# Sliding-window attention with a gated feed-forward block: the first two pairs of query tiles worked by halves of their heads, and the written order planned again

## The chip, the cores and the metric

The kernel runs on one NeuronCore of a Trainium2 chip. The core has five engines that each follow their own list of instructions: TensorE (PE in the profile; PEld is its weight load), VectorE (DVE), ScalarE (ACT), GpSimd (POOL) and SyncE (SP), which here only issues transfers. The metric is the device time of one execution in microseconds. Eleven executions of the kernel before have a median of 258.07 us, from 257.2 to 260.35.

## The reference

The reference is causal attention over q, k, v of shape (4 batches, 8 heads, 768 positions, 64), followed by a gated feed-forward block. Heads 0, 2 and 6 see every earlier position. The other five see the first 4 positions (the sinks) and a window of 64.

```python
scores = scale * np.matmul(q, k.transpose(0, 1, 3, 2))
# mask: causal for heads 0, 2, 6; causal and (sink or window) for the others
a = np.exp(scores - np.max(scores, axis=-1, keepdims=True))
a = a / (np.sum(a, axis=-1, keepdims=True) + 1e-09)
x = np.matmul(a, v)                     # (4, 8, 768, 64) -> (3072 tokens, 512)
g = x @ w_gate                          # 512 -> 1536
out = (g / (1 + np.exp(-g)) * (x @ w_val)) @ w_out
```

## The kernel before

**Tiles and pairs.** A query tile is 128 positions of one batch with all 8 heads; there are 24. Tiles come in 12 pairs, because one load brings 256 positions: load q*n*, k*n*, x*n* (x is v) are 512 KB each. A pair goes through a cast to 16 bits (`cast`, tasks cq, ck), transposes on TensorE (`transposes`, tasks tr*n*.0 for q and tr*n*.1 for k) and evacuations from PSUM (`evacq` and `evack`, tasks evq and evk) into `qT` and `kT`. From pair 5 on, transfers that transpose (dq, dk) take the place of TensorE's transposes.

**A tile.** Each tile has units of scores (sc*t*.*u* on TensorE), an exponential on ScalarE (ex), for tiles from 4 on a multiplication with a mask (mask, VectorE or GpSimd), matmuls with the values for the odd heads and then for the even ones (val*t*.1, val*t*.0), a division by the row sum (rc and nm, VectorE), and a transposition into `xt` (xtr and xe, or from tile 8 on a transfer, xdma).

**Feed-forward.** Four tiles make a group of 512 tokens, six groups in all. For each of 12 blocks j of 128 hidden units there are four matmuls with the gate weights (`gate`, L778, task gate*g*.*j*), a tanh on ScalarE, one VectorE instruction that makes silu's first part (`stt1`, L788), four matmuls with the value weights (L778, task vals*g*.*j*), and one VectorE instruction that multiplies both (`stt2`, L795). Group 0 does its blocks 0 to 3 in two halves of 256 tokens. The output product (L813) follows. Weights are loaded by pieces of 512 KB (g, v and o, 0 to 5), and cast (tasks wc); piece v1 holds the value weights of blocks 2 and 3.

**PSUM.** The ring `gv` has three buffers. Both kinds of feed-forward matmul write there: a gate block gives its buffer back when `stt1` has read it, a value block when `stt2` has. So VectorE's pace sets when TensorE may start the next block. In the first two pairs k's transposes and some scores and value products use `gv` too. The rings `tr`, `sc` and `av` have one buffer each, and `raw`, where loads land, has 14.

**The order.** Nothing is scheduled when the kernel is built. Tasks are declared with what they need; `ORDER`, a string of two-digit numbers, gives the one sequence in which all are issued, and `WAYS` the engine of each task that has a choice. Both were written by a planner that isn't in the file. Each engine takes its tasks strictly in that sequence, SyncE its transfers too. Numbers from 3700 up are spare matmuls (`warm`) that compute nothing.

**Places.** `load` L311, `cast` L377, `transposes` L428, `evacq` L443, `evack` L448, `tasks_of_pair` L624, `tasks_of_tile` L687. The helpers `copy` (L175 on ScalarE, L177 on the others) and `recast` (L181, VectorE's cast, written as a reduction over one element) record most moves, so their lines gather several tiles.

Of the kernel before, what the change touches and what calls it, by code (L numbers as in the profile page):

```python
# [16 lines left out]
    "000802041L1M1T091O1V1Nxl1Y1W1U1Z1X1a0A01xj1b1c0B1p1t1q0C1Q0E1R1P1r031f0D1d2527262D280i1u1s1S1y2G"  # L17
    "0j2j1g2E1exi1i1h1n2H1o212I2F1j2A1k1l1v221z2J2K1w1x201mxh2L2M23290F24xh2p2N2O2P2q2V2W2r2Q2R102B9F"
    "2C2S9G159j2X2Z9Z2a112k0p2s169k2b9H0H2t2Y2c2d9a9b9P2x9l2e2T2y3Q9m9c2U2h9n0o2u2i9Q2v369R0I0k9o9d9p"
    "05063W3Y0G133A129q9I9J9S9T3B0q9r9s3D073X3E9K9L9M3R3Z3a9N30319e3C0K189O9t3M3b9f9y0n2w2m2l9u9g9v3c"  # L20
    "329h3e33192z9zA0A10L499i3F349U2o354F0t3f2n3G0l0JA29w1H2fAN3d9V3p0m9W4A4G4H9x3H1I0s3h37AO3IAS3J3i"
    "383KAT3t3u9XAP394I3L9YAQ4J3j3k1B3SA83N3V4K0r0M3O3g3TAR3lAV1E3m4L0NAUA9AA3zAW3n3oAI403wAJAD3xA30O"
    "3P41421F3q3U3v43AK443r3sALAEAFAM0v4NA41C3y45461K4WA54p4O4qAG4oAHA60PA747480yAB4Z4yBk4a2gACBlBmBn"
    "4PBVBoBWBG4c4wAwBXBHBI4d0xAzAx4Q4RAyB00u4BBfBgBhBiBjBJBK4M4C4S4TBQBR4xB6B7BS4v0w4f4gAu4E0zB8BTAr"
    "0R4l4DAs4z5014BUAtB1B24U4V0S17AX4YAv52Ba53Bb4uB31D1ABYAY0Y4b4e4X5D1G4r4h5758B90QBZ4i5G1JAZ5W5X5Z"
    "4jAaBABLB45e515H5JBM5V5K544kBc0TAc4mB5BB555IAdAe5f4s59BN5LBC56BO5M5N5cAf5d0U5A5BAhAi5O5P5C5E4t5Y"
    "5Q5RBEBPAg5g635F5S5h5iAjAk5r4nBDBd0X5T5U62615a5s5tAmAnAoBFCd5b6iAbCeAp6ABeCgCfCh69CYCZCOBpCPCQ5o"
    "5y6B68Aq0WBqBrCa5jBsCRCS5p6F6GC9CbCcCA5k5qBuCB0V0a6C6DCs6O6HBvCt6X6Y5uCu6h6l6gAl6m5vCvCw6UCiBt66"
    "6V6o6p5l6n5m64CjCkCl6q6E6RCJ6SCK6d5w5xCLCECm6I6J6TBw655n5zD26K0h8d600ZCT7PBx7XByBzCF6WD30b6u6v67"
    "6LC07W6MD46P6NCMCUCNCV6Q6r6sC16Z6aC2C3D5CHD66x6y6bCG6eCW757TCICx6cCX7879Cn7OCC6j6k7BC46t71Cy0gC5"  # L30
    "C6C7CzCDD0Co726fEA0d7C7N7V7UEBD7Cp0cCqCr6z70D1C8D86w737AEF747v8283EC7REGEH7g7hE0E57jE6E17tE27u7k"
    "D9DAEIEJE77D767I7J0f7SEDEEE8E97Q7EDgDR7FDhDSDT7GDCDD7H7YE37K7L0e7Z8a8h7lDEDiDbDeE481DcDU807i7q87"
    "7mDdDFDG88EKDH7nDV8YDy77DI7a7bDfDJDvDK7cELEMDLDw847o7pDMDxDq858A8B7rDW8G7z8c8MDNDO8Z8NDz7s7MDrDs"
    "DPDtDu868P8i7dDjDk7eDX8fDZ8QDYDa7w8JENEODl7x8gDm8CEPDnDo7fFSDpFTDB8D8KFU8V89FIFJ8EF3FL8pFKEyFMEz"
    "F0EQERES8H8F8eF1F88qF28OF9FA8mFDFEF4EU8L7y8R8S8nEVETF5DQFVFW8j8xF6F78kEW8lEX8r8s8T8U8WFGFFFH8oFc"
    "FdFNFOFP93948IEZEaFf8b8tEY8u90FeFg8X91EtEuEbEcEvFQ8vFB8w8z8y92EwFC989A99FXExFY969BEeFZ97Eo95Ep9C"
    "Fa9D9EFbEfEqEgEhFRErEsEjEkEmElEnGuGvGwGBGxGyFhGGGHGIEiGCGDGkGlGmFiGnGoFjGEGFGQFkGRGsFmFnGpGSEdGq"
    "GrGtFoFpFqG1G2GVGWG4G3G5G6GXFrFsGYGZGaGbGcFtFuGJGKG7GLGMFwFlG8FvG9GdGAFxGTGNGeGUGOGPGfFyGgFzGhGi"
    "GzH0GjH1G0H4H5H6H9HAHBHEHFHGH7H2H3H8HCHDHJHHHIHKHL"
)  # L40
WAYS = (
    "000000000000000000000000000000000000000000000000000000000000002022222222222222222210201212101000"
    "011000000100000000000000010001100202212210110100100001000000000000000200022220001101000000000000"
    "020000000000000010012220220000000100000000000100000000100000000012210220110000100000000011000100"
    "000000021010210210000000000000000002000010000000000002200120000000100000000001000010001210200000"
    "001001000000200001000000000000222020100000010010000000021000000100000000020122000000001000000000"
    "010000210020002200000000010000000200010000000000101222022000000100000000000000001000000000000000"
    "000000000000000000000000000000000000000000000000000000000000000000000000000000000000010000000000"
    "000000000000000000000000000000000000000000000000000000000000000010000000001000000000000000000000"
    "000000000000000000000000000000000000000000000000000000000000000000000000000000000000000000000000"  # L50
    "000000000000000000000000000000001000000000100000000000000000000000000000000000000000000000000000"
    "000000000000000010000000000000000000000000000000000000000000000000000000000000000000000000000000"
    "10000000000000000010"
# [52 lines left out]
def kernel(  # L106
# [204 lines left out]
    def load(kind, n):  # L311
        r = buf("raw", [128, 1024], FP, "raw")
        landed[kind, n] = r
        if kind in "qkx":
            b, pi = QP[n]
            sl = slice(pi * 256, (pi + 1) * 256)
            nc.sync.dma_start(  # L317
                out=r.rearrange("p (h x) -> p h x", h=H),
                in_={"q": q, "k": k, "x": v}[kind][b, :, sl, :].rearrange(
                    "h (p j) d -> p h (j d)", j=2))  # L320
        elif kind == "o":
            nc.sync.dma_start(
                out=r.rearrange("p (a n) -> p a n", a=2), in_=wod[:, 2 * n:2 * n + 2, :])
        else:
            nc.sync.dma_start(  # L325
                out=r.rearrange("p (a n) -> p a n", a=4),
                in_=(wgd if kind == "g" else wvd)[:, :, n * 256:(n + 1) * 256])

    T_load, T_iss = {}, {}
    for kd, n in ([(kd, n) for n in range(NP) for kd in "qkx"]  # L330
                  + [(kd, n) for kd in "gvo" for n in range(6)]):
        T_iss[kd, n] = P.add(f"load {kd}{n}", ["SP"], (lambda kd=kd, n=n: load(kd, n)),
                             takes=["raw"])
        T_load[kd, n] = P.lands(T_iss[kd, n])
# [42 lines left out]
    def cast(n, kd, x):  # L377
# [8 lines left out]
        if n not in hqs:  # L386
            h = buf("hq", [128, 2, 1024], FH, "hq")
            hqs[n] = [h[:, 0].rearrange("p (j r x) -> p j r x", j=2, r=2),
                      h[:, 1].rearrange("p (k a x) -> p k a x", k=2, a=4)]
        if kd == "k":  # L390
            ks = slice(0, 2) if x is None else slice(x, x + 1)
            recast(T_c[n, kd, x],
                 hqs[n][1][:, ks].rearrange("p k a (s d) -> p k s a d", s=2),
                 r.rearrange("p (k s r) j d -> p k s (r j) d", r=2, s=2)[:, ks])
            return
        js = slice(0, 2) if x is None else slice(x, x + 1)
        recast(T_c[n, kd, x],
             hqs[n][0].rearrange("p j r (k d) -> p k r j d", d=64)[:, :, :, js],
             r[:, :, js].rearrange("p (k r) j d -> p k r j d", r=2))
# [28 lines left out]
    def transposes(n, w):  # L428

        ring = "gv" if w and n < 2 else "tr"  # L430
        tr = buf(ring, [128, 4, 2, 2, 64] if w else [128, 2, 4, 128], FH, "tr")
        for j in range(2):
            for p in range(4):
                if w:
                    nc.tensor.transpose(tr[:, p, :, j, :], hqs[n][1][:, p // 2, p % 2 * 2 + j],
                                        ident)
# [4 lines left out]
        trs[n, w] = tr  # L441

    def evacq(n, s, x, ps):  # L443
        c = slice(s * 64, s * 64 + 64)
        copy(T_ev[n, s][x], qT[n % 2][c, s, ps].rearrange("c p j n -> c j p n"),
             trs[n, 0][c, :, ps])

    def evack(n, x, ps):  # L448
# [3 lines left out]
        copy(T_ev[n, 2][x],  # L452
             kT[b % 2][:, 2 * pi:2 * pi + 2].rearrange("c m k r x -> c (k r) m x")[:, ps],
             trs[n, 1][:, ps].rearrange("c p m j n -> c p m (j n)"))
# [169 lines left out]
    def tasks_of_pair(n):  # L624
# [5 lines left out]
        for kd in "qk":  # L630
            free = xqk and kd == "q"
            cs[kd] = []
            for x in range(2) if n < 2 or free else [None]:
# [3 lines left out]
                    deps=[T_load[kd, n]] + ([T_fill3] + T_dq.get(n - 1, []) if free else []),  # L637
# [24 lines left out]
        for w in range(xqk, 2 - xk):  # L662
            ring = "gv" if w and n < 2 else "tr"
            tr = P.add(f"tr{n}.{w}", ["PE"], (lambda n=n, w=w: transposes(n, w)),
                       deps=cs["qk"[w]], takes=[ring], after=[T_warm])
            cut = [slice(2, 4), slice(0, 2)] if n < 2 else [slice(0, 4)]
            evs = []
            if w:
                for x, ps in enumerate([slice(1, 4, 2), slice(0, 4, 2)] if n < 2 else cut):
                    evs.append(P.add(f"evk{n}.{x}", ["ACT", "DVE"],  # L670
                                     (lambda n=n, x=x, ps=ps: evack(n, x, ps)),
                                     deps=[tr] + older))
                T_ev[n, 2] = evs
            else:
                oldq = [x for t in (2 * n - 4, 2 * n - 3) if n > 1 for x in T_sc_of[TILES[t]]]
                T_ev[n, 0], T_ev[n, 1] = [], []
                for x, ps in enumerate(cut):
                    for s_ in range(2):
                        T_ev[n, s_].append(P.add(
                            f"evq{n}.{s_}{x}", ["ACT", "DVE"],  # L680
                            (lambda n=n, s_=s_, x=x, ps=ps: evacq(n, s_, x, ps)),
                            deps=[tr, T_fill0] + oldq))
                        evs.append(T_ev[n, s_][-1])
            P.uses(tr, ring, *evs)
            P.uses(first, "hq", tr)
# [247 lines left out]
```

## Time and profile before

| what | value |
|---|---|
| median of 11 executions | 258.07 us (257.2 to 260.35) |
| the profiled execution, its own time | 257.66 us |
| its span, first to last instruction | 255.5 us |
| granted TensorE clock | 1.0 throughout |
| TensorE matmul busy | 247.2 us (97%) |
| VectorE, ScalarE, GpSimd busy | 166.0, 139.2, 97.3 us |
| bytes moved | 42.52 MB; 290 to 333 GB/s from 6 to 51 us |

The profiled execution's time is 2.16 us above its span, and 0.4 us under the median. A matmul's end is modelled, so TensorE's busy time also holds waits between matmuls; how much work it gets through is better read from the number of matmuls in a stretch. The row of VectorE in the slices has its high digits from the fifth slice to the tenth, 25 to 64 us.

### The profile page before, as it was taken

To read this page: it belongs to the slowest core of one execution; us is meant where nothing else is said; L and a number is where in the kernel's file an instruction comes from. 1 tells how busy PE (TensorE), PEld (TensorE's weight loads), DVE (VectorE), ACT (ScalarE), POOL (GpSimd) and SP (SyncE) were. 2 spreads that over 40 slices of the span, in tenths; PEclk is the share of its full clock that TensorE was granted. 3 is DMA by queue.
4 is the path that set the end of the run, shared out by engine and by line. 5 is a ranking of instruction groups with operands and counts; after the bars stand their busy time and mean duration, and the time that the engine had idled before them with its cause. 6 is when DMAs were issued, how large, how long until landed. Compare 5 with 4: busy or idle time off the path is not lost.

```text
span 255.5 us, 4866 instructions
## 1 busy us (share of the span) xinstructions
PE 247.2 (97%) x1813; PEld 136.8 (54%) x1813; DVE 166.0 (65%) x344; ACT 139.2 (54%) x230; POOL 97.3 (38%) x124
## 2 busy tenths in 40 slices
PE   7988999999999999999999999999999999999994
PEld 3666767665455554555555555555555554444442
DVE  3577999998889463578955636476575866455510
ACT  2878898866557474486646743663645323133101
POOL 6474789592763463445511720503142100000000
PEclk9999999999999999999999999999999999999999
DMA  7999999989949989997988852361321121031034
GB/s 188 290 318 319 320 323 333 299 258 236 319 89 249 232 142 176 268 216 185 245 201 218 176 117 64 79 127 45 75 53 39 21 64 41 0 83 41 19 93 97
DMA packets 80535, 42.52 MB, mean 166 GB/s; under 512 B 32768, under 2 KB 76032, under 8 KB 80512
## 3 DMA queue, kind: packets, MB, share of 16 engines
q1 hardware_dynamic: 80352, 42.09, 67.2%
q8 instruction: 14, 0.23, 0.4%
q10 hardware_dynamic: 160, 0.13, 0.2%
q14 instruction: 9, 0.07, 0.1%
HBM read 28.31 MB, written 6.29 MB: 135 GB/s over the span
## 4 chain that ended last, share of the span: by engine, by line
PE 78%; DMA 8%; DVE 6%; SPq 5%; issue 1%; POOL 0%; ACT 0%; DVEq 0%
PE gv L778 44%; PE o_ps L813 21%; PE sc L547 7%; PE av L577 4%; SPq L317 4%; DMA raw<-in_moe_w_val_dram 4%; DMA xt<-xb 3%; DVE h L795 1%; DVE vt L181 1%; SPq L325 1%; DVE xb L594 1%; DMA out_dram<-o_sb 1%; DVE m L255 1%; DVE sil L788 1%; PE xtr L610 0%
## 5 line engine op out<-in xcount | busy, mean ns | idle before, releaser
L557 ACT ACTIVATE e<-sc 128x1024 f16<-128x1024 f32 (+3 forms) x71 | 62.3, 880 | 35.7 <-PE sc L547 34.8
L778 PE MATMUL gv<-xt,wv_sb 128*128 128x512 f16 (+1 forms) x304 | 72.7, 368 | 0.8 <-POOL wv_sb L177 0.6
L778 PE MATMUL gv<-xt,wg_sb 128*128 128x512 f16 (+1 forms) x304 | 72.6, 368 | 0.6 <-DMA xt<-xb 0.3
L813 PE MATMUL o_ps<-wo_sb,h 128*128 128x512 f16 (+2 forms) x300 | 70.0, 371 | 0.0
L788 DVE SCALAR_TENSOR_TENSOR sil<-sig,gv 128x512 f32<-128x512 f32 (+1 forms) x76 | 49.3, 654 | 31.0 <-ACT sig L784 30.3
L784 ACT ACTIVATE sig<-gv 128x512 f32<-128x512 f32 (+1 forms) x76 | 43.0, 575 | 47.4 <-PE gv L778 46.5
L795 DVE SCALAR_TENSOR_TENSOR h<-sil,gv 128x512 f16<-128x512 f32 (+1 forms) x76 | 49.2, 655 | 15.8 <-PE gv L778 14.6
L565 POOL TENSOR_TENSOR e<-e,m 128x1024 f16<-128x1024 f16 (+1 forms) x19 | 35.7, 1877 | 44.2 <-ACT e L557 37.3
L813 PEld LDWEIGHTS <-h 128*128 128x128 f16 x300 | 28.1, 98 | 28.5
L778 PEld LDWEIGHTS <-wv_sb 128*128 128x128 f16 x304 | 28.2, 98 | 28.0 <-POOL wv_sb L177 1.0
L778 PEld LDWEIGHTS <-wg_sb 128*128 128x128 f16 x304 | 28.6, 98 | 27.2 <-DMA xt<-xb 0.8
L547 PE MATMUL sc<-qT,kT 128*128 128x256 f16 (+1 forms) x276 | 37.5, 257 | 0.0
L547 PEld LDWEIGHTS <-kT 128*128 128x128 f16 x276 | 25.2, 98 | 14.6 <-DVE kT L177 0.6
L577 PEld LDWEIGHTS <-e 128*128 128x128 f16 x472 | 19.9, 97 | 8.3 <-ACT e L557 1.1
L577 PE MATMUL av<-vt,e 128*128 128x65 f16 x472 | 22.5, 193 | 0.8 <-ACT xb L592 0.4
L175 ACT COPY o_sb<-o_ps 128x512 f32<-128x512 f32 (+1 forms) x17 | 9.8, 579 | 20.9 <-PE o_ps L813 20.9
L594 DVE TENSOR_TENSOR xb<-av,rc 128x256 f16<-128x256 f32 x45 | 19.1, 423 | 1.8 <-DMA xt<-xb 0.3
L582 DVE RECIPROCAL rc<-av 128x4 f32<-128x4 f32 x48 | 8.5, 178 | 14.3 <-PE av L577 13.7
L177 POOL CAST vt<-raw 64x512 f16<-64x512 f32 x22 | 14.5, 659 | 7.1 <-DMA raw<-in_v_dram 6.2
L177 POOL CAST hq<-raw 128x1024 f16<-128x1024 f32 (+1 forms) x14 | 12.7, 913 | 9.0 <-DMA raw<-in_k_dram 5.5
L177 DVE COPY o_sb<-o_ps 128x512 f32<-128x512 f32 (+1 forms) x8 | 5.1, 639 | 13.5 <-DMA out_dram<-o_sb 10.6
L565 DVE TENSOR_TENSOR e<-e,m 128x640 f16<-128x640 f16 (+1 forms) x19 | 12.4, 657 | 0.2 <-ACT e L557 0.2
(55 smaller groups left out, 136.0 us busy)
## 6 DMA issues: line engine op xcount, KB each, us to landing
raw<-in_q_dram SPq DMA_DIRECT2D x12, 512.0 KB, 5.2
raw<-in_k_dram SPq DMA_DIRECT2D x12, 512.0 KB, 7.3
raw<-in_v_dram SPq DMA_DIRECT2D x12, 512.0 KB, 6.8
out_dram<-o_sb SPq DMA_DIRECT2D x46, 128.0 KB, 2.4
raw<-in_moe_w_gate_dram SPq DMA_DIRECT2D x6, 512.0 KB, 7.4
raw<-in_moe_w_val_dram SPq DMA_DIRECT2D x6, 512.0 KB, 7.9
raw<-in_moe_w_out_dram SPq DMA_DIRECT2D x6, 512.0 KB, 5.8
xt<-xb SPq DMA_TRANSPOSE x16, 2.4
```

The lines of the kernel that those rows point to most:

```text
L177: ENG[task.way].tensor_copy(out=dst, in_=src)
L317: nc.sync.dma_start(out=r.rearrange("p (h x) -> p h x", h=H), in_={"q": q, "k": k, "x": v}[kind][b, :, sl, :].rearrange("h (p j) d -> p h ...
L547: nc.tensor.matmul(sc[c // 4][:, c % 4:c % 4 + n, :], weights, moving, start=first, stop=last)
L557: nc.scalar.activation(out=e[:, 0:n], in_=whole_sc.pop((t, u))[:, 0:n], func=AF.Exp, scale=scale)
L565: ENG[task().way].tensor_tensor(out=ev, in0=ev, in1=mm, op=ALU.mult)
L577: nc.tensor.matmul(av[:, n, 0:65], ee, vv, start=(m == 0), stop=(m == len(bl) - 1))
L594: nc.vector.tensor_tensor(out=xbs[t][:, :, odd, :], in0=av[:, :, 0:64], in1=rc.to_broadcast([128, 4, 64]), op=ALU.mult)
L778: nc.tensor.matmul(ps, wsb[:, kk, j * 128:(j + 1) * 128], xt[:, kk, c[0]:c[1]], start=(kk == 0), stop=(kk == 3))
L784: nc.scalar.activation(out=sg[g, j, c], in_=gs[g, j, c], func=AF.Tanh, scale=0.5)
L788: nc.vector.scalar_tensor_tensor(out=sl[g, j, c], in0=sg.pop((g, j, c)), scalar=1.0, op0=ALU.add, in1=gs.pop((g, j, c)), op1=ALU.mult)
L795: nc.vector.scalar_tensor_tensor(out=hs[g, j][:, c[0]:c[1]], in0=sl.pop((g, j, c)), scalar=0.5, op0=ALU.mult, in1=vs.pop((g, j, c)), op1=A ...
L813: nc.tensor.matmul(o_open[g, tt, x], hs[g, j][:, tt * 128:(tt + 1) * 128], wo_sb[:, j, lo:hi], start=(j == 0), stop=(j == NJ - 1))
```

## The change

Pairs 0 and 1 are worked by halves of their heads. Half x=0 is the odd heads, x=1 the even ones (before, q's casts were cut by position and k's by pairs of heads, and there was one PSUM tile for all eight transposes of an operand).

- The loads of q0 and k0 become two loads of 256 KB each, into one raw buffer.
- Each cast of these pairs takes one half; q's and k's transposes go four at a time into a PSUM tile of their own, in ring `tr` or `gv` (`tr_ring`).
- An evacuation reads its own half's PSUM tile alone: three per half and pair, six per pair as before.
- A unit of scores waits for the evacuations of those halves that it uses (`k_deps(unit)`), not for all.
- `ORDER` and `WAYS` are new throughout. Planned with loads taken to land late, they change the sequence of nearly all tasks, and the engine of many. Among others: in VectorE's list the cast of q0's odd half stands ahead of the clearing of `qT` (fill); in GpSimd's the clearing of `hqz` (fill3) stands second; x0 is loaded after q1; and g1 before g0.

```diff
 ORDER = (
-    "000802041L1M1T091O1V1Nxl1Y1W1U1Z1X1a0A01xj1b1c0B1p1t1q0C1Q0E1R1P1r031f0D1d2527262D280i1u1s1S1y2G"
+    "000A081N0B1Q04xj1d1P1M0103091O021b1Y1e1V1W1a1Zxi1h1i1X0D291c1f1g1v1w2A0C1t1R1r1U1S2H1s1T0E2I2J2B"
...
-    def load(kind, n):
-        r = buf("raw", [128, 1024], FP, "raw")
-        landed[kind, n] = r
+    def load(kind, n, x=None):
+
+        if (kind, n) not in landed:
+            landed[kind, n] = buf("raw", [128, 1024], FP, "raw")
+        r = landed[kind, n]
...
+            hs_ = slice(0, H) if x is None else slice(1 - x, H, 2)
             nc.sync.dma_start(
-                out=r.rearrange("p (h x) -> p h x", h=H),
-                in_={"q": q, "k": k, "x": v}[kind][b, :, sl, :].rearrange(
+                out=r.rearrange("p (h x) -> p h x", h=H)[:, hs_],
+                in_={"q": q, "k": k, "x": v}[kind][b, hs_, sl, :].rearrange(
                     "h (p j) d -> p h (j d)", j=2))
...
+        if kd in "qk" and n == 0:
+            ts = []
+            for x in range(2):
+                ts.append(P.add(f"load {kd}{n}.{x}", ["SP"],
+                                (lambda kd=kd, n=n, x=x: load(kd, n, x)),
+                                takes=[] if x else ["raw"], after=ts[:1]))
+            T_iss[kd, n], T_load[kd, n] = ts[0], [P.lands(t) for t in ts]
+            continue
...
-    def transposes(n, w):
-
-        ring = "gv" if w and n < 2 else "tr"
-        tr = buf(ring, [128, 4, 2, 2, 64] if w else [128, 2, 4, 128], FH, "tr")
+    def transposes(n, w, x):
+
+        ps = range(4) if x is None else range(2 - 2 * x, 4 - 2 * x)
+        tr = buf(tr_ring(n, w, x), [128, 4, 2, 2, 64] if w else [128, 2, 4, 128], FH, "tr")
...
+    def tr_ring(n, w, x):
+        return "tr" if x is None or w == x else "gv"
...
+            for x in range(2) if n < 2 else [None]:
+                ring = tr_ring(n, w, x)
+                tr = P.add(f"tr{n}.{w}.{x}", ["PE"], (lambda n=n, w=w, x=x: transposes(n, w, x)),
+                           deps=[cs["qk"[w]][x or 0]], takes=[ring], after=[T_warm])
...
-        k_deps = [x for kt in range(i // 2 + 1) for x in T_ev[QP.index((b, kt)), 2]]
-        k_deps += T_ev[n, 0] + T_ev[n, 1]
+        def k_deps(unit):
+            halves = sorted({p < 2 for p, hh, c, kt in unit[0]})
+            parts = [(QP.index((b, kt)), 2) for kt in range(i // 2 + 1)] + [(n, 0), (n, 1)]
+            return [x for m, w in parts
+                    for x in ([T_ev[m, w][h] for h in halves] if m < 2 else T_ev[m, w])]
...
-                       deps=k_deps + k_sinks + added, takes=[score_ring(t, u)])
+                       deps=k_deps(unit) + k_sinks + added, takes=[score_ring(t, u)])
```

## The prediction

> **What bounds the kernel now.** I read the page's totals and slices first, then the chain of waits, then busy time by stage, then VectorE's groups and one moment of the timeline.
>
> ```profile
> PE 247.2 (97%) x1813; PEld 136.8 (54%) x1813; DVE 166.0 (65%) x344; ACT 139.2 (54%) x230; POOL 97.3 (38%) x124
> ...
> DVE  3577999998889463578955636476575866455510
> ```
>
> TensorE looks full, but its bars also hold waits. The chain gives its true pace, and the one long wait of the front:
>
> ```profile
> 14.06 9.70 DMA raw<-in_moe_w_val_dram
> 23.82 1.05 POOL wv_sb L177
> 24.91 1.05 PE gv L778 x8
> ...
> 57.84 3.45 PE gv L778 x16
> ```
>
> Sixteen matmuls of 512 columns in 3.45 us are 0.216 us each; starts in the trace give 0.109 for 256 columns, 0.055 for 128 and 0.029 for the value products of 65. The program's list weighted so is 234.3 us of TensorE work without the spare matmuls. I call **lag** the start time of a matmul less the work listed ahead of it. The lag only grows, and the span is 234.3 plus the last lag plus the tail. The first value block of group 0 (vals0.3) starts at 24.91 with 11.65 us of work ahead: lag 13.3. It is 15.3 at 52 us and 17.1 at 251; some 4 us of tail follow. So after 25 us only 3.8 us are lost, and 2.0 of these between 25 and 52.
>
> ```profile
> 20.00:25.00 5.00, 4.41 (x58) 3.52 (x57) 4.22 (x12) 3.87 (x7) 2.14 (x3) 1.00 1.13 325
> 25.00:30.00 5.00, 4.78 (x45) 3.73 (x46) 4.08 (x14) 3.73 (x7) 3.25 (x4) 1.00 1.16 313
> 30.00:35.00 5.00, 5.00 (x48) 3.53 (x46) 4.74 (x12) 4.99 (x9) 3.73 (x6) 1.00 1.14 324
> 35.00:40.00 5.00, 4.82 (x53) 3.25 (x50) 4.82 (x12) 4.47 (x10) 4.71 (x4) 1.00 1.13 327
> 40.00:50.00 10.00, 10.00 (x114) 6.89 (x112) 9.52 (x22) 8.17 (x13) 8.39 (x12) 1.00 1.13 318
> 50.00:60.00 10.00, 10.00 (x88) 5.83 (x86) 9.45 (x20) 7.07 (x11) 7.74 (x8) 1.00 0.86 232
> ```
>
> The columns are PE, PEld, DVE, ACT, POOL, clock, transfers. From 30 to 60 us VectorE (third) is 95% busy, and the transfers run at 313 to 327 GB/s until 50 us. These two, not TensorE, set the lag.
>
> ```profile
> 51.58 0.68 DVE L788 SCALAR_TENSOR_TENSOR sil<-sig,gv 128x512 f32<-128x512 f32 x1
> ...
> 52.52 1.03 PE L778 MATMUL gv<-xt,wv_sb 128*128 128x512 f16 x4
> ```
>
> Here a value block starts 0.26 us after the VectorE instruction that freed its `gv` buffer: VectorE is that close behind the bound.
>
> **The change part by part.**
>
> *Halved loads.* SyncE issues two transfers more; an issue into an empty queue took 0.46 and 0.57 us. The four halves land when q0 and k0 did, the last at about 6.8 us. Halving can gain only if TensorE takes the first half alone. It doesn't: its list begins with k's even half, landing third, and then k's odd half. q's even half is cast on GpSimd behind mkdiag (2.28, from 1.25), fill3 (1.80), mkfar (1.41) and fill1 (0.3), so at 7.05 to 7.65. fill (2.38) now stands behind the cast of q0's odd half (5.05 to 5.74) and ends at 8.1. Two evacuations of 0.42 follow, and the first scores come at 9.0; before, the first scores came at 9.17 and the first on `kT` at 9.45. Gain 0.2 to 0.4 us, on scores alone.
>
> In this trace 512 KB land every 1.81 us while five to eight transfers are in flight, so whatever a transfer costs by itself is not paid in a row. The page "DMA: Bandwidth & Descriptors" of the Trainium skill (section "Anatomy of one DMA — SWDGE (gpsimd) path") puts a fixed cost of about 2 us on each transfer, for transfers that GpSimd issues; two more, paid in a row, would make my sum 263.6 instead of 259.6. The row decides.
>
> *Front's supply.* x0 lands fourth, at 10.4 instead of 8.64, x1 at 14.1 instead of 15.84, g1 at 15.6. Tile 0's values need x0: 1.8 us later, 10.4 plus a q1 cast already done plus two casts of 0.68 is 11.85 for the first value product, against 11.24. But v1 is eleventh of the 512 KB pieces in both lists, with the same ten ahead of it, so it lands at about 23.7 again; its cast (1.02 on ScalarE for 1.04 on GpSimd) ends at 24.85. The TensorE work ahead of vals0.3 is 11.65 us in both lists. What the front gains before 24.9 is therefore given back there. Bounds: 0 and +0.5.
>
> *VectorE up to there.* It now casts half of q0, half of q1, three of four parts of x0 and g1, and does eight normalizations of tiles 0 to 3 instead of five. Followed by hand: q1's last evacuations 13.35, tile 1's last norm 16.5, g1's cast 18.2, first gate block 19.3 (before 19.81), pair 2's evacuations 21.6, first stt1 22.0, pair 2's kT 24.2, third stt1 25.6. Before, the first stt2 starts at 25.56. So in both kernels VectorE enters the next stretch at 25.6 (bounds 24.9, the end of v1's cast, and 26.5).
>
> *VectorE from 25.6 us.* Compare two value blocks with the same 37.2 us of TensorE work ahead: before, vals0.9 (52.52 us), after, vals0.11. Before, its buffer is freed by a stt1 that is the tenth full-size stt of the list; after, by stt2 of block 8, the tenth as well. What VectorE has to do from 25.6 us up to there:
>
> ```profile
> L788 DVE SCALAR_TENSOR_TENSOR sil<-sig,gv 128x512 f32<-128x512 f32 x9 | 6.0, 678 | 0.2 <-ACT sig L784 0.2
> ...
> L181 DVE TENSOR_REDUCE vt<-vt 2x330 f16<-2x330 f16 x6 | 2.9, 482 | 0.0
> ...
> L177 DVE COPY qT<-tr 64x1024 f16<-64x1024 f16 x2 | 1.4, 684 | 0.0
> ...
> L181 DVE TENSOR_REDUCE hqz<-raw 128x512 f16<-128x512 f32 x1 | 0.7, 680 | 0.0
> ```
>
> Common to both: ten full stt (0.68), thirteen half-size (0.41), two xe (0.42), the nine mask fills (3.0), six norms with reciprocal (0.60) and one small sink copy (0.2): 6.8 + 5.3 + 0.8 + 3.0 + 3.6 + 0.2 = 19.7. Before adds six masks (three at 0.70, three at 0.49), two evacuations (0.68) and two copies of value sinks (a pair of 0.48, so 0.97): 3.6 + 1.4 + 1.9 = 6.9, in sum 26.6; measured, from 25.56 to 52.26, 26.7. After adds four masks (2.6), three evacuations (2.0), three sink copies (2.9) and two casts of x3 (1.4): 8.9, in sum 28.6, and 28.8 with the idle share of before. VectorE is done at 54.4, the block starts at 54.45, and the lag there is 17.2 instead of 15.3: **+1.9 us**. Bounds: +1.0 with the start at 24.9 and no idle, +3.0 with the start at 26.5 and more idle. I take +1.9, since the same count reproduces the row of before to 0.1.
>
> *GpSimd and ScalarE there.* The masks moved off VectorE wait on GpSimd behind v2's cast: v2 lands 17th, at 33.6 as before, cast to 34.6, a mask (1.4 to 2.4) to 36.0 to 37.0, for val4.0 with 21.9 ahead: lag 14.1 to 15.1, hidden behind VectorE. Later masks and casts of GpSimd (g5 by 41.5, 27.4 ahead) give 14.1. If VectorE were quick, these would bind at about 15. ScalarE has 3 us less up to 60 us: hidden either way.
>
> *After 60 us.* VectorE has some 8 us more over the whole run, in stages where it is 60 to 70% busy: cost 0, bounds 0 and +0.7. SyncE's queue is reordered; the transposes of tile 10 are issued behind those of tile 11, as tile 9's were behind tile 10's, and before, the wait for such a transfer cost 0.44 us at 96.5. A TensorE that is 1.9 us later meets these with more room: -0.5 to +0.5, taken as 0. Matmuls and tail are the same.
>
> *Sum.* 257.66 + 0 (front) + 1.9 + 0 = **259.6 us**, on the profiled execution, which lies 0.4 under the median of 258.07.
>
> **The rivals.**
>
> *Slower still.* VectorE's in-order waits add up and group 3's order loses too: +3.0 + 0.7 gives 261.4. For it: GpSimd at 8.4 of 10 us in 40 to 50 is tight as well. Against: before had only 1.8 us idle on VectorE in 25 to 50.
>
> *No change.* The stretch costs +1.0, and the later losses of 1.8 us (96.5, 129.5, 201 us) shrink by half, as TensorE arrives later: 258.3. For it: those waits are short, each under 0.5. Against: VectorE is not what 0.44 of them waits for.
>
> *Faster, the other side.* VectorE is not the limit in the new list, because its front work is done while transfers land. Then the landings bind: v2's cast at 34.64 against 20.15 us of work ahead is lag 14.5, 0.8 less than 15.3, and the losses that end with VectorE's results at 129.5 and 201 us, 0.6 together, go too: 256.3. It decides if VectorE has finished stt2 of block 8 by 51.7 us, 2.7 us before my count. Against it: VectorE waits for the first landing until 5.05, with fill no longer hidden there.
>
> *The halves do nothing.* By the first part this holds of the front in any case, and is inside all of these.
>
> **How the numbers follow.** Likeliest, 259.6, own range 258.8 to 260.6: 0.48. Slower still: 0.15. No change: 0.22. Faster: 0.15. A difference of 0.5% (1.3 us) is about what a measurement here can tell from none, so slower begins at 259.4 and faster ends at 256.8. Two thirds of the likeliest and all of the slower rival give 0.47 slower; faster 0.15; the rest 0.38. The range from 256.4 to 261.4 leaves out some 0.1 at either end.
>
> **What would show it.** Right: v1's value block starts at 24.9 to 25.4 in both; VectorE over 95% busy from 26 to 55 us; the block with 37.2 us ahead starts near 54.4; the span is about 257.4. Wrong: that block at 52 or sooner (faster rival), or v1 landing away from 23.7, which moves all that follows; a lag that grows by more than 2.5 after 60 us would be the order's later part.

## The result

The kernel after takes **261.16 us**, median of 12 executions (260.13 to 263.15). The kernel before, measured beside it, takes 257.84 us (47 executions). The ratio is 1.0113, with a 95% interval of 1.0083 to 1.0143: slower, by 2.9 us by the ratio and 3.3 by the medians. The executions of before fall into two groups, 33 from 257.0 to 258.3 us and 14 from 259.3 to 260.6, and its median belongs to the faster one. The profiled execution of after took 261.83 us with a span of 259.6, 4.1 us more than the span of before.

The totals and VectorE's slices of the page of after:

```profile
PE 245.7 (95%) x1811; PEld 136.2 (52%) x1811; DVE 175.4 (68%) x349; ACT 136.7 (53%) x207; POOL 91.9 (35%) x133
...
DVE  2698998997798678779786777464665666644501
```

TensorE has the same number of matmuls less two spare ones. VectorE is fuller at the start, as the list said. Where the 4.1 us arise is read from the lag, defined as in the prediction:

| place (TensorE work ahead) | lag before | lag after | lost so far |
|---|---|---|---|
| first value block vals0.3 (11.65 us) | 13.3 | 14.4 | 1.11 |
| block with 37.2 us ahead | 15.3 | 20.7 | 5.36 |
| last matmul | 17.1 | 21.2 | 4.12 |

So 1.1 us come in the front, 4.3 in the stretch up to 58 us, and 1.2 are given back after it.

**The front.** The chain of waits of after (start, duration, what) leads from the last transfer of q0 through GpSimd's cast into one unbroken row of VectorE's instructions:

```profile
2.34 6.15 DMA raw<-in_q_dram
8.54 0.62 POOL hq L177
9.21 0.41 PE tr L450 x4
9.64 0.43 DVE qT L177
10.09 0.42 DVE qT L177
10.53 0.43 DVE qT L177
10.97 0.42 DVE kT L177
11.40 0.59 DVE hq L181
11.99 0.58 DVE vt L181
12.59 0.68 DVE vt L181
13.30 0.68 DVE vt L181
```

Before, that chain ran through the transfers up to v1 and its cast; here v1 isn't in it. q0's even half lands at 8.49 us, 1.7 us later than all of q0 and k0 had before. That is the latest of the nine profiles with these loads (6.97 is the earliest), and this execution is 0.67 us above the median of its kernel, so the 1.1 us of the front are this profile's and not what every execution pays.

**The stretch.** Busy time by stage, after (columns as in the prediction):

```profile
20.00:25.00 5.00, 4.76 (x61) 3.84 (x60) 3.87 (x10) 4.41 (x7) 2.26 (x4) 1.00 1.14 323
25.00:30.00 5.00, 4.98 (x50) 3.67 (x51) 4.52 (x14) 3.07 (x6) 3.45 (x6) 1.00 1.16 311
30.00:35.00 5.00, 4.51 (x42) 3.17 (x40) 4.62 (x14) 4.85 (x7) 3.83 (x6) 1.00 1.09 324
35.00:40.00 5.00, 4.94 (x60) 4.07 (x58) 4.74 (x11) 4.33 (x8) 3.97 (x4) 1.00 1.13 326
40.00:50.00 10.00, 7.76 (x69) 4.60 (x67) 8.57 (x20) 6.31 (x10) 7.28 (x12) 1.00 1.13 314
50.00:60.00 10.00, 8.63 (x108) 5.60 (x106) 9.72 (x19) 6.67 (x11) 7.44 (x9) 1.00 0.54 160
```

Between 40 and 50 us TensorE does 69 matmuls where it did 114, and nobody is full: VectorE 8.57, ScalarE 6.31, GpSimd 7.28 of 10. That is the picture of engines that wait for each other. The timeline of after shows the longest of these waits (the bracket holds an engine's idle time and who ended it):

```profile
40.55 0.42 DVE L611 TENSOR_TENSOR xb<-av,rc 128x256 f16<-128x256 f32 x1
...
41.33 0.69 DVE L177 COPY qT<-tr 64x1024 f16<-64x1024 f16 x1
...
42.12 1.01 ACT L175 COPY qT<-tr 64x1024 f16<-64x1024 f16 x1 [2.76 <-DVE qT L177]
...
43.02 1.02 ACT L574 ACTIVATE e<-sc 128x1024 f16<-128x1024 f32 x1
...
44.09 0.60 PE L564 MATMUL sc<-qT,kT 128*128 128x256 f16 x5 [1.71 <-ACT e L574]
```

Pair 4's q has two evacuations that read one PSUM tile. The new `WAYS` gives evq4.1 to VectorE and evq4.0 to ScalarE, and in the built program ScalarE's waits for VectorE's, which was issued first. VectorE reaches it only at 41.33, after a sink copy, a norm and an stt2. ScalarE stands idle for 2.76 us, the exponential ex6.0 stands behind it, and the scores sc6.1 need the one buffer of ring `sc` that ex6.0 frees. TensorE's lag jumps by 1.87 us at sc6.1. Before, both evacuations of pair 4 were VectorE's and both of pair 3 ScalarE's.

Both evacuations also write into the same `qT`, so that could be the reason instead. The first pairs decide between the two. In before, one PSUM tile held all of q0's transposes, and evacuations on different engines waited for each other (timeline of before):

```profile
8.65 0.42 DVE L177 COPY qT<-tr 64x512 f16<-64x512 f16 x1 [1.11 <-ACT qT L175]
...
9.10 0.58 ACT L175 COPY qT<-tr 64x512 f16<-64x512 f16 x1 [0.48 <-DVE qT L177]
```

In after, the halves of q0 have PSUM tiles of their own, and VectorE and ScalarE write the one `qT` at the same time (timeline of after):

```profile
9.64 1.32 DVE L177 COPY qT<-tr 64x512 f16<-64x512 f16 x3 [1.98 <-PE tr L450]
...
9.87 0.58 ACT L175 COPY qT<-tr 64x512 f16<-64x512 f16 x1 [2.06 <-PE tr L450]
```

So the wait comes with the shared PSUM tile. A split isn't always paid for: pair 3's q is split in after too, but VectorE comes to its share at 34.22, long after ScalarE's (30.69 to 31.70).

The second jump, 1.40 us, is at val6.1. The same view, 8 us on:

```profile
49.10 2.12 POOL L582 TENSOR_TENSOR e<-e,m 128x1024 f16<-128x1024 f16 x1 [1.56 <-ACT e L574]
...
49.67 2.10 DVE L582 TENSOR_TENSOR e<-e,m 128x1024 f16<-128x1024 f16 x1
...
51.83 0.42 PE L594 MATMUL av<-vt,e 128*128 128x65 f16 x8 [1.24 <-DVE e L582]
```

VectorE's mask6.0 takes 2.10 us, though a mask of this shape takes 0.68 elsewhere in the same trace. GpSimd's mask7.0 had started 0.57 us ahead of it and ends at 51.22, and VectorE's ends 0.55 later. The page "SBUF — State Buffer" of the Trainium skill (section "SBUF: two separate sides") says that VectorE and GpSimd share one pair of ports, which whoever starts first holds for its whole instruction, where VectorE reads two operands from SBUF and GpSimd reads SBUF too. The trace agrees: 2.10 for 0.68.

The block that the prediction placed at 54.4 us starts at 57.88, again right behind the VectorE instruction that freed its buffer (timeline of after):

```profile
57.14 0.69 DVE L814 SCALAR_TENSOR_TENSOR h<-sil,gv 128x512 f16<-128x512 f32 x1
...
57.88 0.81 PE L797 MATMUL gv<-xt,wv_sb 128*128 128x512 f16 x3
```

### The profile page after: what moved, and what is told of

Same layout as the page of the kernel before. It is cut to its first block, busy times and chain, and to the rows that moved or that the text cites. A ratio compares the mean times of both kernels' runs of the same rounds, so it can differ in the third digit from the quotient of the medians.

```text
span 259.6 us, 4845 instructions
## 1 busy us (share of the span) xinstructions
PE 245.7 (95%) x1811; PEld 136.2 (52%) x1811; DVE 175.4 (68%) x349; ACT 136.7 (53%) x207; POOL 91.9 (35%) x133
## 4 chain that ended last, share of the span: by engine, by line
PE 82%; DVE 9%; DMA 2%; ACT 2%; issue 1%; SPq 1%; POOL 0%; DVEq 0%; ACTq 0%
PE gv L797 44%; PE o_ps L832 24%; PE sc L564 8%; PE av L594 5%; DMA raw<-in_q_dram 2%; DVE vt L181 2%; ACT e L574 2%; DVE sil L807 2%; DVE qT L177 1%; DVE xb L611 1%; DVE e L582 1%; DVE h L814 1%; SPq L320 1%; PE tr L450 1%; DVE kT L177 0%
## 5 line engine op out<-in xcount | busy, mean ns | idle before, releaser
L582 POOL TENSOR_TENSOR e<-e,m 128x640 f16<-128x640 f16 (+1 forms) x20 | 34.4, 1723 | 40.2 <-ACT e L574 39.2
L797 PEld LDWEIGHTS <-wg_sb 128*128 128x128 f16 x304 | 28.6, 98 | 26.8 <-issue 0.2
L611 DVE TENSOR_TENSOR xb<-av,rc 128x256 f16<-128x256 f32 x48 | 20.4, 424 | 1.6
L175 ACT COPY o_sb<-o_ps 128x512 f32<-128x512 f32 (+1 forms) x18 | 10.4, 579 | 19.4 <-PE o_ps L832 19.4
L177 POOL CAST vt<-raw 64x512 f16<-64x512 f32 x22 | 13.6, 622 | 10.5 <-DMA raw<-in_v_dram 9.3
L177 POOL CAST hq<-raw 128x1024 f16<-128x1024 f32 (+1 forms) x13 | 12.1, 937 | 13.7 <-DMA raw<-in_k_dram 7.5
L177 POOL COPY vt<-vt 2x330 f16<-2x330 f16 x14 | 6.3, 453 | 23.0 <-PE av L594 22.6
L582 DVE TENSOR_TENSOR e<-e,m 128x1024 f16<-128x1024 f16 (+1 forms) x18 | 13.1, 726 | 0.9 <-ACT e L574 0.9
```

Of the source, the lines that this page charges most:

```text
L175: nc.scalar.copy(out=dst, in_=src)
L177: ENG[task.way].tensor_copy(out=dst, in_=src)
L582: ENG[task().way].tensor_tensor(out=ev, in0=ev, in1=mm, op=ALU.mult)
L611: nc.vector.tensor_tensor(out=xbs[t][:, :, odd, :], in0=av[:, :, 0:64], in1=rc.to_broadcast([128, 4, 64]), op=ALU.mult)
L797: nc.tensor.matmul(ps, wsb[:, kk, j * 128:(j + 1) * 128], xt[:, kk, c[0]:c[1]], start=(kk == 0), stop=(kk == 3))
```

## The experiments

Most edits move single tasks to another engine, in the line that reads `WAYS`; the sequence stays as it is. "Growth" is the lag at the block with 37.2 us ahead less the lag at vals0.3: 2.0 us before, 6.3 after, both from one profile each.

**a1_whole_loads: the kernel after, with q0 and k0 loaded whole.**

```diff
 def load(kind, n, x=None):
+        if x == 1:
+            return
...
-            hs_ = slice(0, H) if x is None else slice(1 - x, H, 2)
+            hs_ = slice(0, H)
```

> The changed kernel with q0 and k0 loaded whole again (k0 first, 512 KB each); order, engines, casts, transposes and evacuations by halves stay. In the changed kernel the last half of q0 landed at 8.49 us, where the whole of k0 had landed at 6.83 before, and the first value block of group 0 started 1.1 us later than before (26.03 for 24.91). Theory 'late halves': with whole loads q0 is there at about 6.85, the first value block starts at 25.0 to 25.3, and the time falls by 0.8 to 1.1 us to about 260.2. Rival 'given back': what the front gains is lost again at later waits on other engines, time 261.0 to 261.4. Rival 'chance': the slow landing was an accident of one execution, and the whole loads land no sooner relative to other executions; time unchanged.

Measured: 263.53 us (261.57 to 263.73, 6 executions), ratio 1.0178 (1.0136 to 1.022). k0 landed at 4.94 and q0 at 6.75, and still the first scores that use `qT` and `kT` came at 10.81 us (10.55 in after, 9.07 in a2). The timeline says why:

```profile
6.78 0.69 DVE L181 TENSOR_REDUCE hq<-raw 128x512 f16<-128x512 f32 x1 [6.78 <-DMA raw<-in_q_dram]
...
7.51 0.48 DVE L278 MEMSET qT<- 64x512 uint32 x1
...
9.40 0.48 DVE L279 MEMSET qT<- 64x512 uint32 x1
9.90 1.31 DVE L177 COPY qT<-tr 64x512 f16<-64x512 f16 x3
```

VectorE's cast of q0's odd half now waits for all of q0, and fill (2.38 us) stands behind it. So this run doesn't price the halves alone, and it tests none of its three theories. It shows that this list needs them: the early half is what lets fill run while the other half travels. It showed one thing more. At sc6.1 TensorE waited as in after, and then its clock fell (busy time by stage, the sixth value is the clock):

```profile
43.00:44.00 1.00, 0.10 (x1) 0.10 (x1) 0.29 (x1) 1.00 (x2) 0.20 (x2) 0.90 1.16 360
44.00:45.00 1.00, 1.00 (x8) 0.82 (x8) 0.64 (x1) 0.38 (x2) 0.66 (x2) 0.50 1.02 334
```

It stood at 0.50 for 3.4 us. Five of the six executions have a mean clock of 0.991 to 0.993 and took 263.45 to 263.73; the one at 1.0 took 261.57.

**a2_evq4_act: evq4.1 from VectorE to ScalarE.**

```diff
-            t.way = t.ways[int(w)]
+            t.way = {"evq4.1None": "ACT"}.get(t.name, t.ways[int(w)])
```

> The changed kernel with both evacuations of q of pair 4 on ScalarE (evq4.1 moved from VectorE). In the changed kernel ScalarE's evq4.0 waits for VectorE's evq4.1 of the same PSUM tile, which stands behind a norm and a sink copy; the exponential of sc6.0 stands behind it on ScalarE, and TensorE's sc6.1 waited 1.87 us for that. Theory 'cross wait': with both on one engine ScalarE doesn't wait, sc6.1 starts at most 0.3 us late, and the time falls by 1.2 to 1.9 us, to 259.3 to 260.0. Rival 'VectorE's work' (the step of the prediction): VectorE's list is the bound right behind, the wait only hid it; lag at the block with 37.2 us of work ahead falls by 0.7 us or less (evq4.1 is 0.68 us), time 260.5 to 261.0.

Measured: 259.69 us (259.29 to 260.29, 12 executions), ratio 1.0053 (1.0032 to 1.0074). Timeline:

```profile
38.11 2.02 ACT L175 COPY qT<-tr 64x1024 f16<-64x1024 f16 x2
...
40.03 1.02 ACT L574 ACTIVATE e<-sc 128x1024 f16<-128x1024 f32 x1
...
41.10 0.60 PE L564 MATMUL sc<-qT,kT 128*128 128x256 f16 x5 [0.26 <-ACT e L574]
```

ScalarE does both evacuations in a row, with no wait, and sc6.1 loses 0.42 us instead of 1.87. The block with 37.2 us ahead starts at 55.00, with a lag of 17.8. One task moved is worth 1.5 us, and 1.45 of these lie at sc6.1 itself: the wait between the two engines is shown as the largest single cause.

**a3_mask7_dve: mask7.0 from GpSimd to VectorE. a4_casts_x3_act: two casts of x3 (cx3.1) from VectorE to ScalarE.** Both are made in the kernel after, in the same line:

```diff
+            t.way = {"mask7.0": "DVE"}.get(t.name, t.ways[int(w)])
...
+            t.way = {"cx3.1.0": "ACT", "cx3.1.1": "ACT"}.get(t.name, t.ways[int(w)])
```

> The changed kernel with the mask of unit 0 of tile 7 on VectorE instead of GpSimd. In the changed kernel VectorE's mask6.0 took 2.10 us instead of 0.69, from 49.67 to 51.77, while GpSimd's mask7.0 ran from 49.10 to 51.22, and TensorE's val6.1 waited 1.40 us for it. Theory 'held by GpSimd': mask6.0 takes 0.7 to 1.2 us (a cast of GpSimd may stand in mask7.0's place), the wait of val6.1 falls under 0.5 us, and the time by 0.4 to 1.0 us, to about 260.5. Rival 'the operand, not the neighbour': mask6.0 takes 2 us again. Rival 'VectorE's work': mask7.0 adds 0.69 us to VectorE, time 261 or more.

> The changed kernel with the two casts of x3 that stand on VectorE (cx3.1.0, cx3.1.1, 0.68 us each) on ScalarE. Theory 'VectorE's work' (the step of the prediction): 1.4 us less for VectorE ahead of stt2 of block 8, so the block with 37.2 us of TensorE work ahead starts 0.7 to 1.4 us sooner than 57.88, time 259.9 to 260.6. Rival 'single waits': the lag comes from waits at 42 and 50 us, which the casts at 47.4 and 52.4 don't cause; time 260.9 to 261.3. Rival 'ScalarE': 1.2 us more on ScalarE ahead of exponentials delays scores; 261.5 or more.

Measured: a3 262.3 us (261.66 to 263.49, 6 executions), ratio 1.0152 (1.0115 to 1.019); a4 261.32 (260.19 to 262.38, 6), ratio 1.0105 (1.0064 to 1.0146). Neither gained in the median. In a3 the growth is 5.8 instead of 6.3, and mask6.0 took 1.45 us, now beside GpSimd's cast of v5; but something at the end cost more than was gained (see b2). In a4 the growth is 5.1; three of its six executions have a mean clock of 0.991 to 0.993 (262.1 to 262.4), and its profile, one of these, shows the clock at 0.50 from 15 to 18.5 us. The other three took 260.2 to 260.6, the times that the theory of VectorE's work named; three executions are a hint and no proof. With the wait at sc6.1 still there (1.87 us in both) and these disturbances, the two runs decide nothing, so both edits were tried again without the wait.

**b1_evq4_casts_act and b2_evq4_mask7: the same two edits on top of a2.**

> Edit: as a2_evq4_act (evq4.1 on ScalarE), and the two casts of x3's odd half (cx3.1.0 and cx3.1.1, 0.68 us each) from VectorE to ScalarE (0.62 each). Theory of VectorE's amount of work: once ScalarE no longer waits for VectorE at evq4, the count of the prediction holds (its block with 37.2 us ahead started at 55.00 there, 54.4 counted), so 1.4 us less on VectorE make that block start at 53.6 to 53.9 and the time 258.4 to 258.8, against 259.69 of a2_evq4_act. Rival (waits between engines, not amounts, set the pace: a VectorE mask held by GpSimd's mask, ScalarE's queue): the block stays at 54.8 to 55.2 and the time at 259.5 to 259.9.

> Edit: as a2_evq4_act, and mask7.0 from GpSimd to VectorE. Theory of the shared hold: in a2_evq4_act VectorE's mask beside GpSimd's took 1.47 us instead of 0.69, and GpSimd's own 2.24; with both on VectorE each takes 0.69 and the wait ahead of val6.1 (1.07 us there) falls to 0.3 to 0.5, so the block with 37.2 us ahead starts at 54.2 to 54.6 and the time is 258.9 to 259.3. Theory of VectorE's amount: 0.69 more work there and 0.78 less hold, so no change, 259.5 to 259.9. Third: GpSimd was the better place, the mask on VectorE delays what stands behind it: 260.2 or more.

Measured: b1 258.83 us (258.43 to 260.08, 12 executions), ratio 1.0022 (0.9991 to 1.0052). The growth falls from 4.7 to 3.8, and the block starts at 54.44 after a front 0.3 us later than a2's. That is 0.9 us of the 1.4 that VectorE was spared, so the amount of VectorE's work binds when the wait is gone. The start expected was missed, the time nearly met.

b2 took 260.36 us (260.12 to 261.22, 7), ratio 1.0098 (1.0062 to 1.0134), which was the third case. Yet inside the stretch it did what the shared hold says. VectorE's masks, by the timeline of b2:

```profile
46.17 0.49 DVE L582 TENSOR_TENSOR e<-e,m 128x640 f16<-128x640 f16 x1
...
47.73 0.68 DVE L582 TENSOR_TENSOR e<-e,m 128x1024 f16<-128x1024 f16 x1
47.84 1.47 POOL L177 CAST wv_sb<-raw 128x1024 f16<-128x1024 f32 x1 [1.78 <-DMA raw<-in_moe_w_val_dram]
...
50.32 0.68 DVE L582 TENSOR_TENSOR e<-e,m 128x1024 f16<-128x1024 f16 x1
```

The first took 1.24 and the second 1.47 us in a2. Here VectorE starts first and it is GpSimd's cast that takes 1.47 instead of 1.03. The growth is 3.95 instead of 4.7. The time went elsewhere: the front was 0.9 later in this profile, and the end was longer. The issues of the last 17 us, in the view of the transfers (tiles, engine, operation, count, size, median us from issue to landing), of b2:

```profile
out_dram<-o_sb ACTq DMA_DIRECT2D x1, 96.0 KB, 3.7
```

and of a2:

```profile
out_dram<-o_sb ACTq DMA_DIRECT2D x1, 96.0 KB, 2.4
```

ScalarE's last two issues take 2.71 us in b2 and 2.86 in a3, the two kernels with mask7.0 on VectorE, and 1.38 to 1.40 in every other kernel of this study.

**b3_before_evq4_split: the wait put into the kernel before.** One of pair 4's two evacuations goes to ScalarE.

```diff
-            t.way = t.ways[int(w)]
+            t.way = {"evq4.10": "ACT"}.get(t.name, t.ways[int(w)])
```

> Edit: the kernel before, with one of its two evacuations of pair 4's q (evq4.10) moved from VectorE to ScalarE, so that the two engines read one PSUM tile, as in the kernel after. VectorE has 0.70 us less. Theory of the cross wait: ScalarE's evacuation waits for VectorE's (39.71 to 40.41 in the trace of before), ends at 41.4, and the exponential ex5.2 behind it, which started at 39.04, starts at 41.4; the scores sc6.2 that need its PSUM tile come 1.3 to 1.6 us later, and the time is 258.7 to 259.6 (part of it given back, since later losses shrink). Rival, that a split over two engines is harmless or good: 257.4 to 258.2.

Measured: 260.6 us (259.05 to 261.82, 12 executions), ratio 1.0098 (1.0066 to 1.0131). The profiled execution is the lowest of the twelve, 259.05 us with a span of 257.0, 1.5 more than that of before. Timeline:

```profile
40.31 1.01 ACT L175 COPY qT<-tr 64x1024 f16<-64x1024 f16 x1 [1.82 <-DVE qT L177]
41.33 0.81 ACT L557 ACTIVATE e<-sc 128x768 f16<-128x768 f32 x1
...
42.19 0.60 PE L547 MATMUL sc<-qT,kT 128*128 128x256 f16 x5 [1.62 <-ACT e L557]
```

VectorE has 0.7 us less to do and the kernel is slower: the lag jumps by 1.78 at sc6.2, where before had no jump. Only 0.3 of it is given back: the last lag is 18.6 for 17.1. That is the theory's range in the profiled execution. The median of all twelve lies 1.5 above that execution and above the range, since six executions took 261.3 to 261.8, three of them at a mean clock of 0.992. What slowed the other three isn't known.

**b4_before_halved_loads: the price of halving.**

```diff
-            nc.sync.dma_start(
-                out=r.rearrange("p (h x) -> p h x", h=H),
+            for hs_ in [slice(1, H, 2), slice(0, H, 2)] if kind != "x" and n == 0 else [slice(0, H)]:
+                nc.sync.dma_start(
+                    out=r.rearrange("p (h x) -> p h x", h=H)[:, hs_],
...
```

> Edit: the kernel before, with the loads of q0 and k0 each issued as two transfers of 256 KB by alternate heads into the same buffer, and nothing else. Theory of the prediction: a transfer in a row of several in flight has no price of its own, k0 lands within 0.2 us of 6.83 and the time stays within 0.4 of the kernel before (257.7 to 258.5). Rival: two more transfers pay for themselves in the row; k0 lands 0.5 to 2 us later, all behind it too, and the time is 258.6 to 260.

Measured: 257.62 us (256.78 to 263.45, 12 executions), ratio 1.0005 (0.9967 to 1.0043). k0 was complete at 7.57 instead of 6.83, which is what the rival named and outside what the theory gave it, but v1 landed at 22.73, not later than the 23.76 of before, and the time is the same. The Trainium skill's fixed cost of some 2 us for each transfer that GpSimd issues (page "DMA: Bandwidth & Descriptors", section "Anatomy of one DMA — SWDGE (gpsimd) path"), which the prediction weighed, isn't paid by two more transfers of SyncE's in this row.

**c1, c2 and c3: all edits, and the front's.** c1 is b1 and b2 together. c2 is the kernel after with three of VectorE's casts in the front on GpSimd. c3 is both.

```diff
 c1
+            t.way = {"evq4.1None": "ACT", "cx3.1.0": "ACT", "cx3.1.1": "ACT", "mask7.0": "DVE"}.get(t.name, t.ways[int(w)])
 c2
+            t.way = {"cx0.0.0": "POOL", "cx0.1.0": "POOL", "wc g1": "POOL"}.get(t.name, t.ways[int(w)])
```

> Edit: as b1_evq4_casts_act (evq4.1 and both casts of x3's odd half on ScalarE), and mask7.0 from GpSimd to VectorE. In b2_evq4_mask7 the lag grew by 3.95 us from the first value block (vals0.3) to the block with 37.2 us ahead, against 4.69 in a2_evq4_act, and yet the time was 0.67 longer: ScalarE's last two issues took 2.71 us there instead of 1.40, as in a3_mask7_dve (2.86). Theory: mask7.0 on VectorE saves 0.7 us in the stretch, and the longer last issues come from where ScalarE's instruction list ends in its 8192-byte fetches (one instruction fewer in those two kernels); here ScalarE has two instructions more again, so the issues take 1.40, the growth is 3.0 to 3.2 and the time 258.0 to 258.4. Rival (the mask on VectorE itself makes the end longer): issues of 2.7 and 259.4 or more. Third, nothing gained: growth 3.8 as in b1_evq4_casts_act, 258.7 to 259.0.

> Edit: the kernel after, with two of VectorE's casts of x0 (cx0.0.0, cx0.1.0, 0.69 us each) and its cast of g1 (1.21) moved to GpSimd, which has gaps of 2.7 us ahead of k1 and of 0.9 ahead of q2. Theory that VectorE's chain from the last half of q0 sets the front: in the profiles so far vals0.3 starts 17.5 to 17.8 us after q0's even half lands, whether v1 lands at 23.2 or at 24.0; with 2.6 us less on VectorE it starts 1.2 to 1.6 after v1's landing, 16.2 to 17.2 behind q0's half, and the time falls from 261.16 to 260.0 to 260.7. Rival, the prediction's own reading (v1's landing binds the front): nothing is gained, 260.9 to 261.5.

> Edit: c1_evq4_casts_mask7 and c2_front_relief together. If the front's chain, the cross wait, the held mask and VectorE's amount are the four causes, and each gives back its own: 258.2 less 0.5 to 1.0 for the front, 257.2 to 257.7, level with the kernel before or 0.3 us ahead of it. Rival, that with these gone the landings of v1 and v2 bind the same lag: 258.0 to 258.6, no better than c1_evq4_casts_mask7.

Measured: c1 257.95 us (257.61 to 258.86, 12 executions), ratio 0.9992 (0.9963 to 1.0021). The growth is 3.1, as expected, ScalarE's last issues take 1.40, and four moved tasks have brought the kernel level with before. Busy time by stage and, from the timeline, the block with 37.2 us ahead, both of c1:

```profile
40.00:50.00 10.00, 9.71 (x103) 6.18 (x104) 9.47 (x22) 8.74 (x14) 6.71 (x11) 1.00 1.15 319
```

```profile
53.59 1.02 PE L797 MATMUL gv<-xt,wv_sb 128*128 128x512 f16 x4
```

TensorE is back at 103 matmuls in those 10 us (69 in after), and VectorE at 95% (86% in after): it does its work instead of waiting.

c2 took 260.74 us (260.49 to 261.9, 6), ratio 1.0102 (1.0052 to 1.0152). This is 0.42 below after in the median, with overlapping intervals, and its 17.27 us from q0's half to vals0.3 lies just above the range named; by time alone it decides nothing. The starts decide. In the profiles vals0.3 starts close to the later of two times, q0's even half plus 17.55 us and v1's landing plus 1.5. Both offsets are fitted, the first to after and b2, the second to a2, a3 and b1:

| kernel | q0's half landed | v1 landed | later of the two | vals0.3 started |
|---|---|---|---|---|
| after | 8.49 | 23.99 | 26.04 (half) | 26.03 |
| b2 | 8.08 | 23.21 | 25.63 (half) | 25.61 |
| b1 | 7.42 | 23.54 | 25.04 (v1) | 25.07 |
| a2 | 7.00 | 23.21 | 24.71 (v1) | 24.73 |
| a3 | 7.07 | 23.39 | 24.89 (v1) | 24.88 |
| c1 | 7.16 | 23.20 | 24.71 (both) | 24.87 |
| c2, VectorE relieved | 7.66 | 23.43 | 25.21 (half) | 24.93 |
| c3, VectorE relieved | 7.14 | 23.51 | 25.01 (v1) | 24.98 |

In c2 the half no longer sets it: the start is 1.50 behind v1. That is one profile. a4, whose clock was at 0.50 from 15 to 18.5 us, doesn't fit: it started at 26.88 for 25.12. c3 took 258.04 us (257.53 to 259.09, 12), ratio 0.9975 (0.9939 to 1.0012): no better than c1, as the rival had it. Its half landed early (7.14), as c1's did (7.16), so there was little for the front's edits to win. No kernel here is shown to beat the one before.

## Why the prediction was right, and where it was wrong

Slower was right, and 261.16 lies inside the whole range, 0.24 us from its upper end. It lies outside the likeliest case's own range (258.8 to 260.6) and nearest to the rival *Slower still* (261.4), which had been given 0.15. The size, 1.5 us for 3.3, was too small, for a reason that the prediction had ruled out. That the time stayed inside the whole range was partly luck: all three terms of the sum fell outside their bounds, and the last one the other way.

*Halved loads.* That the transfers themselves cost nothing in the end is shown by b4. That all four halves land "when q0 and k0 did, the last at about 6.8 us" failed: in the profiles of the kernels with halves the last came at 7.0 to 8.5. The first scores came at 10.10 in after and at 8.61 in a2, for 9.0 predicted.

*Front's supply.* v1 landed at 23.2 to 24.0, as said, and the gain was given back, as said, where the half landed early. The bound of +0.5 was too narrow: when the half is late, VectorE's chain ends later than v1's cast, and the profile of after lost 1.1. *VectorE up to there:* the third stt1 ended at 26.7 in after and at 25.4 in a2, 25.6 predicted.

*VectorE from 25.6 us.* The count was right about an amount that it wasn't alone in setting. With the wait between the engines taken out (a2) the block starts at 55.00 with a lag of 17.8, for 54.4 and 17.2 predicted. With 1.4 us of casts less (b1) 0.9 us of growth go, with mask6.0 unheld too (c1) another 0.7. In the kernel itself VectorE was not over 95% busy from 26 to 55 us: 90% from 25 to 50 (22.45 of 25), with the held mask counted as busy. That the count came within 0.1 us of the row of before was partly luck. It took three masks of 128x640 at 0.49 each, where the row of before has a mean of 0.90:

```profile
L565 DVE TENSOR_TENSOR e<-e,m 128x640 f16<-128x640 f16 x3 | 2.7, 902 | 0.0
```

The 1.2 us that are missing so, and 1.3 us of idle time in that stretch, were made up by instructions that overlap in the trace: their times sum to 28.6 us in a stretch of 26.7.

*GpSimd and ScalarE there* is **the step that failed**. "ScalarE has 3 us less up to 60 us: hidden either way" looked at amounts. ScalarE had less to do and made TensorE wait, since two evacuations that share a PSUM tile had been given to two engines. a2 takes 1.5 us away with it, and b3 puts 1.5 us into the kernel before. The trace of before showed such waits, 1.11 and 0.48 us in q0's evacuations, and the change takes them away in pairs 0 and 1; pair 4 still shares one PSUM tile, and the list of after put evq4.1 on VectorE ahead of evq4.0 on ScalarE, with ex6.0 behind it. The same step missed the held masks: two of the three in the row above took 1.18 and 1.05 us, beside casts of GpSimd, and the third 0.48.

*After 60 us* was costed at 0, bounds -0.5 and +0.7. After lost 0.6 there and before 1.8, so 1.2 us came back, more than the bounds allowed. That is what the rival *No change* said, and more strongly.

*The sum.* Predicted for the profiled execution: 0 in the front, +1.9 in the stretch, 0 after it. Measured: +1.1, +4.3 and -1.2. Of the 4.3 in the stretch the wait is 1.6 (growth 6.3 in after, 4.7 in a2), x3's casts are 0.9 (3.8 in b1) and the hold 0.7 (3.1 in c1). What is left is 1.1 (c1 for the 2.0 of before), and no run takes it away. The casts and this rest are 2.0 together, about the 1.9 that was counted for VectorE's work, but only the casts' part is shown to be that. By the ratios to the kernel before (1.0113, 1.0053, 1.0022 and 0.9992), after to a2 is 1.5 us, a2 to b1 0.8 and b1 to c1 0.8: all of the loss. The intervals of neighbours overlap in the last two steps; there the growths carry the reading.

*The rivals.* Slower still (261.4) had the right time by the wrong way: not VectorE's waits adding up and a loss in group 3, but a wait of ScalarE for VectorE. Faster fell: it needed stt2 of block 8 by 51.7 us, and this ended at 57.83 in after and at 53.54 in c1, whose growth is still 3.1 for the 2.0 of before.

## What to carry to other kernels

When work moves between engines, go through what shares a buffer as well as what each engine has to do: two reads of one PSUM tile on two engines can become a wait, and its price is paid by what stands behind the waiting instruction, here an exponential that a one-buffer ring was waiting for. Where VectorE multiplies two operands from SBUF, ask what GpSimd runs at that moment. And one median can hide a gain: the casts and the mask gave none in the medians of a3 and a4, where a longer end and a lower clock in some executions covered it, and 0.9 us each in b1 and c1, tried with the larger wait out of the way.

## What the runs showed of the hardware

- **The end of ScalarE's list.** With mask7.0 on VectorE, ScalarE's list has one instruction fewer in a3 and b2 (327 in the trace, waits included, for 328 in after and a2). In both, ScalarE's last two issues take 2.86 and 2.71 us instead of 1.40. The trace has packets of 8192 bytes on the queue that the page calls instruction: in a2 the last but one begins at 251.71, ahead of the issues at 252.89; in b2 it begins at 253.69, after the issues began at 253.28, and in a3 at 254.93, after 254.37. c1 has mask7.0 on VectorE too, but two more instructions on ScalarE, and its issues take 1.40. So the mask is not the cause; that the fetch falls into the last issue is, by these times, the likely one.
- **Half clock after short waits.** In a1 the clock fell to 0.50 for 3.4 us after 40 to 44 us, in which matmuls were busy for 2.0 of 4 us, with one wait of 1.7. The same waits at the same place in after left the clock at 1.0 in its profile; 1 of its 12 executions has a mean clock of 0.993 and is the longest, 263.15 us.
- **Order of landing.** With four transfers of 256 KB at the head of the row, the fourth landed anywhere from 6.97 to 8.49 us in nine profiles of the same loads.
